# Score columns in token order, one store for four heads, masks on VectorE

## Chip, cores, metric

One core of one Trainium2 chip. The metric is the device time of the whole program in microseconds (us). A run over 1.5% above the fastest of its kernel in the same rounds is called slow, and ratios leave it out.

Engines are named as in the profile: PE is TensorE, PEld its weight load, DVE is VectorE, ACT ScalarE, POOL GpSimd. A store's landing is the time from its issue until its data has arrived. The granted clock is the share of TensorE's full clock that the chip allowed. In the traces it is 1.0 or 0.5 at any moment, and what is given is its mean over a stretch.

## The reference, cut to what matters

```python
# decode step with its gradients: B=2, one query token, 16 KV heads (32 query heads), 4096 keys, Dh=128
xn = layernorm(x)
scores = einsum("bhqd,bhkd->bhqk", q, k) * Dh ** -0.5      # q = xn @ wq
p = softmax(scores);  o = einsum("bhqk,bhkd->bhqd", p, v)   # then @ wo
out = x + attention(xn) + glu(xn)
# the outputs that weigh most: out_2 = dL/dk_cache and out_3 = dL/dv_cache,
# each [2, 16, 4096, 128] bf16; outer products of dscores (or p) with q (or do)
```

The KV caches are read (67 MB) and gradients of the same size are written (67 MB); with the weights and their gradients, 92.5 MB are read and 92.5 MB written.

## The kernel before

Sequence position is split as `(a j c4 cb)`: partition 32a + j of the natural load holds 32 tokens. The scores of the four heads of a group are built in one [128, 256] tile whose columns are (h, c4, j), since the matmul reads the transposed keys `X` at a step of 2 elements within a block of 32 columns j.

```python
def head_scores(src, t, b, g, l, s_ps):                 # t=0: K, t=1: V; l = head 0..3 of group g
    n = nat([P, NCH, Dh], "kv")
    nc.sync.dma_start(n[:].rearrange("p c d -> p (c d)"), src[b, G * g + l])
    X = xtile([P, NCH * Dh], "X")                        # two buffers
    t32(pairs(X[:]), pairs(n[:].rearrange("p c d -> p (c d)")))      # DVE 32x32 transpose, as fp32 pairs
    for be in range(4):
        for cq in range(4):
            nc.tensor.matmul(s_ps[:], lhsT=view(W[t][:], 0, P, (be * G + l) * WW + 24 - 8 * cq, [[1, P]]),
                rhs=view(X[:], 0, P, 2 * cq * Dh + 64 * (be // 2) + be % 2, [[Dh, 2], [8 * Dh, 4], [2, 32]]), ...)

def build_BD(st, b, t):                                  # block-diagonal right-hand sides, cut
    nc.scalar.copy(bd[:], bp[:]...)
    for c in range(4):
        nc.gpsimd.tensor_scalar(BD[t][:, c, :], bd[:], maskc[:, c:c + 1], None, op0=ALU.mult)

okview = out_2.rearrange("b h (a j c4 cb) d -> b h a c4 j (cb d)", a=4, j=32, c4=4)
def unit(A, cq):                                         # outer products: rows x BD, 128 x 1024 to "so"
    m["st"] = [stile([P, G, 8, Dh], "so") for _ in range(2)]          # 1 MB each, four buffers ("st")
    o = [ps_o(), ps_o()]
    ...                                                  # 4 matmuls K=32 into ps_o, evac by ACT or DVE
    if cq == 3:
        for aa in range(2):
            for l in range(G):
                nc.gpsimd.dma_start(oview[b, G * g + l, 2 * A + aa],
                                    m["st"][aa][:, l].rearrange("p c d -> p (c d)"))   # 256 KB
```

The buffers "st" also stage the weight gradients (stw, std, sto, stq). Rows of the softmax, `pr`, and of its gradient, `ds`, feed the outer products (as weights, columns as they stand) and, transposed to `pT` and `dsT`, the contractions with V and K.

## Time and profile before

| | before |
|---|---|
| time, median of the three runs before the prediction | 854.5 us (843 to 862) |
| PE / DVE / ACT / POOL busy | 72 / 42 / 38 / 42% |
| mean granted TensorE clock | 0.641 |
| a so store, issue to landing | 13.8 us (256 KB, 256 of them) |

The prediction below shows the main lines. One more pair will be needed: the span in 40 slices, busy tenths of PE and the granted clock in tenths.

```profile
PE   1885694797956896889786893867749677769532
...
PEclk9876567656775576755655576566866559575555
```

PE falls to 3 to 5 tenths in slices from end to end, and the clock moves between 0.5 and 0.8 in most of them.

### The profile page before, as it was taken

The page shows a single profiled execution, that of the slowest core. Times are in us where ns is not written, and L with a number is a line of the kernel's source. Part 1 is how long each engine was busy: PE and PEld are TensorE (multiplying, and loading weights), DVE is VectorE, ACT ScalarE, POOL GpSimd, SP SyncE. Part 2 cuts the span into 40 slices and gives each one's busy share as a digit, 9 for nine tenths or more (in the row PEclk, how much of TensorE's full clock was granted, in tenths as well). Part 3 has the DMA queues.
Part 4 walks back from the last instruction along what each step waited for, and adds up shares of the span by engine and source line. Part 5 has one row for each costly group of instructions (what it writes and reads, how often), then busy time and mean ns, then how long its engine had stood idle before and what let it go on. Part 6 is the DMA issues. An engine that isn't in the chain of part 4 may idle for free.

```text
span 852.4 us, 14847 instructions
## 1 busy us (share of the span) xinstructions
PE 613.6 (72%) x6297; PEld 306.8 (36%) x6297; DVE 355.2 (42%) x436; ACT 325.6 (38%) x436; POOL 357.1 (42%) x508
## 2 busy tenths in 40 slices
PE   1885694797956896889786893867749677769532
PEld 1543362434422452535242351423424234334100
DVE  8663134414553355324462253414435335352233
ACT  0243443363334444442343451343424434435330
POOL 4543152545334373635342372443536226434402
PEclk9876567656775576755655576566866559575555
DMA  9739598558948799688947798457975789456646
GB/s 314 271 122 246 177 272 277 117 168 255 363 138 266 214 347 300 140 257 264 291 147 214 182 355 265 74 164 251 324 208 157 235 236 329 140 127 135 131 115 155
DMA packets 105050, 186.32 MB, mean 219 GB/s; under 512 B 56300, under 2 KB 71288, under 8 KB 96792
## 3 DMA queue, kind: packets, MB, share of 16 engines
q0 software_dynamic: 76592, 92.89, 44.0%
q1 hardware_dynamic: 28392, 92.49, 29.5%
q8 instruction: 49, 0.80, 0.4%
q14 instruction: 17, 0.14, 0.0%
HBM read 92.48 MB, written 92.48 MB: 217 GB/s over the span
## 4 chain that ended last, share of the span: by engine, by line
DMA 45%; PE 27%; POOL 8%; ACT 8%; issue 5%; DVE 4%; SPq 1%; ACTq 0%; POOLq 0%; DVEq 0%
DMA out_dram<-so 41%; PE ps_o L511 8%; PE ps_sc L474 8%; ACT so L93 6%; POOL out_dram L519 6%; PE ps_m L487 3%; POOL BD L461 2%; DMA kv<-in_A_k_cache_dram 2%; DMA out_dram<-sto 1%; PE ps_m L496 1%; DMA wgu<-in_B_w_up_dram 1%; PE ps_o L379 1%; DVE X L102 1%; ACT std L93 1%; PE ps_m L297 1%
## 5 line engine op out<-in xcount | busy, mean ns | idle before, releaser
L93 ACT CAST so<-ps_o 128x1024 bf16<-128x1024 f32 x212 | 209.5, 1014 | 291.8 <-PE ps_o L511 143.9
L519 POOL DMA_DIRECT2D out_dram<-so x256 | 176.9, 698 | 149.2 <-ACT so L93 76.5
L474 PE MATMUL ps_sc<-X,W 128*128 128x256 bf16 x1024 | 205.9, 349 | 16.2 <-DVE X L102 10.8
L102 DVE STREAM_TRANSPOSE X<-kv 128x2048 f32<-128x2048 f32 x64 | 147.0, 2299 | 84.2 <-PE ps_sc L474 29.7
L474 PEld LDWEIGHTS <-W 128*128 128x128 bf16 x1024 | 108.6, 119 | 98.0 <-issue 65.7
L511 PE MATMUL ps_o<-BD,pr 32*128 32x512 bf16 x256 | 98.5, 559 | 51.1 <-ACT so L93 47.9
L461 POOL TENSOR_SCALAR BD<-bd,maskc 128x512 bf16<-128x512 bf16 x64 | 99.4, 1559 | 64.8 <-ACT bd L458 61.4
L511 PE MATMUL ps_o<-BD,ds 32*128 32x512 bf16 x256 | 86.7, 499 | 55.2 <-ACT so L93 44.8
L90 DVE CAST so<-ps_o 128x1024 bf16<-128x1024 f32 x44 | 53.4, 1214 | 71.7 <-PE ps_o L511 53.3
L379 PE MATMUL ps_o<-dyr,hb 32*128 32x288 bf16 x72 | 20.8, 394 | 46.0 <-ACT std L93 45.9
L511 PEld LDWEIGHTS <-ds 32*128 32x128 bf16 x256 | 15.4, 97 | 81.8 <-issue 78.8
L93 ACT CAST stw<-ps_o 128x1024 bf16<-128x1024 f32 x35 | 34.5, 1015 | 22.4 <-PE ps_o L345 20.8
L352 POOL DMA_DIRECT2D out_dram<-stw x18 | 14.3, 795 | 65.4 <-DMA out_dram<-so 33.6
L487 PE MATMUL ps_m<-kv,pT 128*32 128x128 bf16 x1024 | 40.8, 287 | 0.0
L93 ACT CAST std<-ps_o 128x576 bf16<-128x576 f32 x32 | 19.3, 641 | 56.3 <-DMA out_dram<-so 52.5
L511 PEld LDWEIGHTS <-pr 32*128 32x128 bf16 x256 | 15.5, 101 | 62.9 <-issue 56.0
L487 PEld LDWEIGHTS <-pT 128*32 128x32 bf16 x1024 | 23.5, 120 | 35.6 <-issue 33.9
L384 POOL DMA_DIRECT2D out_dram<-std x9 | 7.7, 859 | 56.5 <-ACT o_sb L490 21.8
L487 PE MATMUL ps_m<-kv,dsT 128*32 128x128 bf16 x1024 | 28.9, 283 | 1.9 <-ACT o_sb L490 1.7
L496 PEld LDWEIGHTS ps_m<-R,o_sb 128*128 128x128 f32 x128 | 24.6, 273 | 12.8 <-issue 10.5
L487 PEld LDWEIGHTS <-dsT 128*32 128x32 bf16 x1024 | 22.8, 127 | 17.4 <-issue 16.5
L496 PE MATMUL ps_m<-R,o_sb 128*128 128x2 f32 x128 | 26.9, 318 | 3.0 <-issue 3.0
(180 smaller groups left out, 575.5 us busy)
## 6 DMA issues: line engine op xcount, KB each, us to landing
out_dram<-so POOLq DMA_DIRECT2D x256, 256.0 KB, 13.8
kv<-in_A_k_cache_dram SPq DMA_DIRECT2D x32, 1024.0 KB, 11.1
kv<-in_A_v_cache_dram SPq DMA_DIRECT2D x32, 1024.0 KB, 11.7
out_dram<-stw POOLq DMA_DIRECT2D x18, 512.0 KB, 9.6
wd<-in_B_w_down_dram SPq DMA_DIRECT2D x9, 576.0 KB, 8.5
out_dram<-std POOLq DMA_DIRECT2D x9, 576.0 KB, 4.2
wo<-in_A_wo_dram SPq DMA_DIRECT2D x4, 1152.0 KB, 11.4
wgu<-in_B_w_gate_dram SPq DMA_DIRECT2D x9, 512.0 KB, 12.7
```

The lines of the kernel that those rows point to most:

```text
L90: nc.vector.tensor_copy(out=out, in_=in_)
L93: nc.scalar.copy(out, in_)
L102: nc.vector.transpose(out, in_)
L297: nc.tensor.matmul(dh[:], lhsT=Wdy[:, k, e, :], rhs=view(Xd[:], 0, P, 64 * k + e, [[D, FC], [2, 32]]), start=(k == 0 and e == 0), stop=(k ...
L352: nc.gpsimd.dma_start(out[0:512, f0:f0 + FS].rearrange("(c p) n -> p c n", p=P), st[:, 4 * w:4 * w + 4])
L379: nc.tensor.matmul(o[aa][:, k, 0:HD2], lhsT=hb[32 * a:32 * a + 32, 0, :], rhs=dyr[32 * a:32 * a + 32, k * HD2:(k + 1) * HD2], start=True, ...
L461: nc.gpsimd.tensor_scalar(BD[t][:, c, :], bd[:], maskc[:, c:c + 1], None, op0=ALU.mult)
L474: nc.tensor.matmul(s_ps[:], lhsT=view(W[t][:], 0, P, (be * G + l) * WW + 24 - 8 * cq, [[1, P]]), rhs=view(X[:], 0, P, 2 * cq * Dh + 64 * ( ...
L487: nc.tensor.matmul(o_ps[32 * cq:32 * cq + 32, :], lhsT=rowsT[:, 4 * h + c4, :], rhs=head[:, 8 * c4 + 2 * cq + h, :], start=(h == 0 and c4 ...
L496: nc.tensor.matmul(t_ps[:, 2 * l:2 * l + 2], lhsT=o_sb[:, l, :], rhs=R40[:, 2 * l:2 * l + 2], start=True, stop=True)
L511: nc.tensor.matmul(o[aa][:, h, :], lhsT=rows[32 * a:32 * a + 32, P * h:P * (h + 1)], rhs=BD[t][32 * a:32 * a + 32, cq, :], start=True, sto ...
L519: nc.gpsimd.dma_start(oview[b, G * g + l, 2 * A + aa], m["st"][aa][:, l].rearrange("p c d -> p (c d)"))
```

## The change

The intent: let the score columns stand in token order, so that row m of a staging tile is token block m. Then one DMA of 1 MB stores four heads ([128 partitions, 4 heads, 2 KB] on both sides), and 256 issues become 64. Token order is made by a strided matmul read for K and a strided transpose write for V. The block masks move from POOL to DVE. (`dve(1.2)` is no instruction: it tells the program's static balance, which shares the evacuations of PSUM between ACT and DVE, of the masks' time.)

```diff
-    okview = out_2.rearrange("b h (a j c4 cb) d -> b h a c4 j (cb d)", a=4, j=32, c4=4)
+    okview = out_2.rearrange("b h (a m cb) d -> b a m h (cb d)", a=4, m=P)       # ovview likewise
@@ build_BD
-            nc.gpsimd.tensor_scalar(BD[t][:, c, :], bd[:], maskc[:, c:c + 1], None, op0=ALU.mult)
+            nc.vector.tensor_scalar(BD[t][:, c, :], bd[:], maskc[:, c:c + 1], None, op0=ALU.mult)
+        dve(1.2)
@@ head_scores
-        t32(pairs(X[:]), pairs(n[:]...))
+        if t == 0:
+            t32(Xf, pairs(n[:]...))
+        else:
+            t32(view(Xf, 0, P, 0, [[1, 4], [P, 16], [4, 32]]), pairs(n[:]...))    # writes fp32 at step 4
-                    rhs=view(X[:], 0, P, ..., [[Dh, 2], [8 * Dh, 4], [2, 32]]),
+                if t == 0:                                                        # reads bf16 at step 8*Dh
+                    r = view(X[:], 0, P, ..., [[Dh, 2], [2, 32], [8 * Dh, 4]])
+                else:
+                    r = view(X[:], 0, P, ..., [[4 * P, 2], [2, P]])
@@ outer_units
-                        for l in range(G):
-                            nc.gpsimd.dma_start(oview[b, G * g + l, 2 * A + aa], m["st"][aa][:, l]...)
+                        nc.gpsimd.dma_start(oview[b, 2 * A + aa, :, G * g:G * g + G],
+                                            m["st"][aa][:].rearrange("p l c d -> p l (c d)"))
@@ softmax (and dscores likewise)
-        t32(pT[:]..., pr[:])
+        t32(pT[:]..., view(pr[:], 0, P, 0, [[P, 2], [1, 4], [4, 32]]))
```

## The prediction

> **What bounds the kernel now.** I read the page first, then the list of waits, then the stores one by one. Engine shares and DMA queues, from the page:
>
> ```profile
> PE 613.6 (72%) x6297; PEld 306.8 (36%) x6297; DVE 355.2 (42%) x436; ACT 325.6 (38%) x436; POOL 357.1 (42%) x508
> ...
> DMA packets 105050, 186.32 MB, mean 219 GB/s; under 512 B 56300, under 2 KB 71288, under 8 KB 96792
> ...
> q0 software_dynamic: 76592, 92.89, 44.0%
> q1 hardware_dynamic: 28392, 92.49, 29.5%
> ...
> DMA out_dram<-so 41%; PE ps_o L511 8%; PE ps_sc L474 8%; ACT so L93 6%; POOL out_dram L519 6%; PE ps_m L487 3%; POOL BD L461 2%; DMA kv<-in_A_k_cache_dram 2%; DMA out_dram<-sto 1%; PE ps_m L496 1%; DMA wgu<-in_B_w_up_dram 1%; PE ps_o L379 1%; DVE X L102 1%; ACT std L93 1%; PE ps_m L297 1%
> ```
>
> No engine is full. The last line is the chain of waits that ended last: 41% of the span (some 350 us) is the landing of the dK/dV stores from the tiles "so". Stores and loads move the same bytes, but the stores take half as much engine time again (44.0% against 29.5%). The list of waits says how this reaches TensorE:
>
> ```profile
> ACT so L93 <- DMA out_dram<-so: 102.4, 19, 13.4
> PE ps_o L511 <- ACT so L93: 92.7, 44, 12.3
> ACT std L93 <- DMA out_dram<-so: 52.5, 7, 11.4
> PE ps_o L379 <- ACT std L93: 45.9, 8, 10.8
> PE ps_o L647 <- ACT so L93: 13.6, 4, 11.6
> ```
>
> The 1 MB staging tiles have four buffers. ACT can't evacuate into one until its store has landed, so PSUM stays full and PE stands. PE's share of it is 92.7 + 45.9 + 13.6 = 152 us of its 239 us of idle (852.4 - 613.6).
>
> Why do the stores land so late? Two stretches answer it (columns: stretch, length, busy time of PE, PEld, DVE, ACT, POOL, granted clock, DMA busy share, GB/s). In the first only so stores were in flight; in the second mainly one stq store, of 1 MB as [128 partitions, 4 runs of 2 KB], which is the very shape that the change gives to so.
>
> ```profile
> 156.00:174.00 18.00, 12.52 (x105) 7.88 (x107) 6.42 (x11) 4.43 (x7) 8.91 (x15) 0.69 0.76 151
> 257.50:260.00 2.50, 2.50 (x17) 1.82 (x17) 1.43 (x3) 0.53 (x3) 2.14 (x4) 0.50 1.01 415
> ```
>
> Beside an idle load queue, so stores move 151 GB/s with the engines 76% busy; stq moves 415. Packet by packet, the 4 KB store packets take a steady 159 ns in the stq stretch; in the so stretch that is still the median, but many take 1 to 2 us. Of the 56300 small packets, 49152 are of 8 bytes, which is 256 so stores x 192, and 192 = 12 x 16: as if 12 of 16 engines got only filler from each so store. The issues agree:
>
> ```profile
> out_dram<-so POOLq DMA_DIRECT2D x256, 256.0 KB, 13.8
> out_dram<-stq POOLq DMA_DIRECT2D x4, 1024.0 KB, 6.7
> ```
>
> A quarter of the bytes takes twice as long. Eight so stores issued together at 154.3 us (2 MB, no loads) had all landed only at 174.9: 20.6 us.
>
> **What the Trainium skill says.** "DMA: Bandwidth & Descriptors", section "Why a DMA increments its semaphore by 16 and not by 1": a copy is spread over the largest k up to 16 that divides the slowest dimension of both patterns. Before, the DRAM side starts with c4 = 4, so k = 4; after, both sides start with 128, so k = 16. The filler count and the 151 against 415 GB/s agree. "SBUF — State Buffer", in "Door 1: The DMA port swizzle": SBUF lines are 16 bytes, and full bandwidth needs at least two hits in a line. K's new matmul read steps 2 KB in its innermost dimension and V's transpose write steps 16 bytes, so both get one. No instruction of the kernel before does either on a long operand, so its trace can't say. "VectorE: DVE Perf Modes", "The perf-mode tier table": tensor_scalar on bf16 in SBUF runs at four elements a cycle. "TensorE: Matmul & The Clock Gate", "Part 1: The HAM clock gate": an idle window of some 3.4 us halves the clock. The trace agrees: score matmuls start 111 ns apart (median) at clock 1.0 and 213 at 0.5, and the mean grant is 0.64.
>
> **The change part by part.** Rows that price it (line, engine, operation, tiles, shape, count, busy us, mean ns, idle before):
>
> ```profile
> L519 POOL DMA_DIRECT2D out_dram<-so x256 | 176.9, 698 | 149.2 <-ACT so L93 76.5
> L461 POOL TENSOR_SCALAR BD<-bd,maskc 128x512 bf16<-128x512 bf16 x64 | 99.4, 1559 | 64.8 <-ACT bd L458 61.4
> L623 POOL DMA_DIRECT2D out_dram<-stq x4 | 3.2, 797 | 5.0 <-DVE stq L90 2.8 <-DVE rowf L752 2.2
> L102 DVE STREAM_TRANSPOSE X<-kv 128x2048 f32<-128x2048 f32 x64 | 147.0, 2299 | 84.2 <-PE ps_sc L474 29.7
> L474 PE MATMUL ps_sc<-X,W 128*128 128x256 bf16 x1024 | 205.9, 349 | 16.2 <-DVE X L102 10.8
> ```
>
> Stores: 256 issues become 64 of 1 MB. POOL loses 256 x 0.698 = 179 us and gets 64 x 0.797 = 51. Landing: two tiles (2 MB) at 400 GB/s take 5.2 us, plus some 3 us of issue and completion: 8 to 9 us in place of 20.6 without loads, perhaps 12 beside them. The direct waits of ACT and DVE for landings add up to 213 us in 37 pieces (102.4, 52.5, 19.7, 16.2, 12.5, 10.1), 5.8 us each, so 10 us off the landing ends nearly all. I take 80% of PE's 152: -120 us.
>
> Masks: 64 x 1.559 = 99 us leave POOL, where stores stood behind them in its queue. On DVE a 128x128 bf16 copy takes 176 ns; another 384 columns at four a cycle add some 0.1, so 0.28 us, 18 us in all, off the path mostly: +5. POOL falls from 357 to about 130 us.
>
> K reads: 512 of the 1024 score matmuls. If one hit a line halves the rate, 213 ns is paid at full clock too. Of the consecutive pairs counted, 371 of 828 ran at clock 1.0: 512 x 0.45 x 0.1 = +23 us of PE.
>
> V writes: 32 transposes of 2.30 us. At half rate they add 32 x 2.2 = 70 us to DVE (42% busy). Mostly hidden; exposed perhaps at the first head of each of eight V phases, 8 x 2.2 = 18, at even odds: +10.
>
> The strided reads in pT and dsT cost nothing: the hT transpose already reads at step 4 (306 ns for 128 columns, against 428 for 256 contiguous).
>
> Clock: fewer long PE gaps should lift the grant from 0.64 to about 0.70. Half of PE's 613 us is rate rather than latency: -25 (estimate).
>
> Sum by PE idle: 854.5 - 120 - 25 + 23 + 10 + 5 = 748. This is the cautious end: it lets PE's busy time stand, though much of it is pipeline tail of matmuls trickling between waits. The chain gives the bold end: 350 us of landings shrink by 60% (-210), its POOL part (8%, 66 us) by 40 us, the costs add 38: 854.5 - 210 - 40 + 38 = 642. In between, leaning to the middle as other waits fill up part of what the chain frees: **695 us**.
>
> **The rivals.** (1) Transfers get no faster, since loads share the engines: landing stays at 10 us and above, gain some 40 us, 815. For it: 74% mean busy share. Against it: that share is mostly stretched packets, and the so stores are slow with no load beside them. (2) PE becomes the bound because K's 2 KB step costs far more than two cycles an element: at 4 times, 512 x 0.3 to 0.45 us = 150 to 230 us, and the result is about 850. Against it: the skill tells of a penalty per line, and a tuned kernel would hardly keep it. (3) DVE becomes the gate: POOL's masks waited 61.4 us for bd in nine waits; in DVE's fixed order (masks now stand between transposes) such a wait holds up the transposes that feed PE. With slow V writes too: 355 + 18 + 70 = 443 us busy, +40, 740. (4) Everything overlaps better and DMA is the floor: 186 MB at the 350 to 400 GB/s of the best stretches is 465 to 530 us, with start and tail of 50 to 70 us: 600.
>
> **Range and chances.** The store effect is measured in this kernel on the same shape, so faster is very likely. The spread comes from how much PE fills up (642 to 748) and from the strides. 80% range 615 to 785; faster by over 2%: 0.94, within 2%: 0.03, slower: 0.03.
>
> **What would show it.** Right: 8-byte packets gone (about 53,000 packets: 105050 - 49152 - 192 x 16), the store queue's share of engine time in us down by a quarter or more, so landing at 6 to 9 us, ACT's waits for landings under 60 us, POOL busy about 130 us, masks near 0.28 us, V transposes 2.3 to 4.6 us, K matmuls spaced at 213 ns at full clock. Wrong: landings still over 11 us (rival 1), K's matmuls above 400 ns apart (rival 2), or DVE waiting for bd while PE waits for X (rival 3).

## The result, and the profile after

The changed kernel took 883.3 us (median of 4 runs, 881.7 to 884.6) against 848.8 (4 runs): ratio 1.050, 95% interval 1.045 to 1.056. It is 5% slower; the prediction had said 695 us, 615 to 785. All ratios here are the mean time of one kernel's fast runs over the mean of the kernel before's fast runs of the same rounds, so they are not quite the ratio of the medians.

The page of the changed kernel, lines as in the prediction:

```profile
PE 798.6 (90%) x6297; PEld 324.7 (37%) x6297; DVE 406.3 (46%) x491; ACT 335.5 (38%) x445; POOL 129.3 (15%) x252
...
PE   2896999979999999979999999979999699997964
...
PEclk9855655565555555566655555556555655558555
...
DMA packets 52823, 185.89 MB, mean 211 GB/s; under 512 B 4076, under 2 KB 19064, under 8 KB 44568
...
q1 hardware_dynamic: 28392, 92.49, 29.6%
q0 software_dynamic: 24368, 92.48, 28.6%
...
PE ps_sc L484 31%; PE ps_o L520 18%; PE ps_m L496 6%; DVE X L102 6%; PE ps_m L505 3%; ACT so L93 3%; PE ps_o L379 2%; PE ps_m L297 2%; PE ps_o L655 2%; PE ps_o L345 1%; PE ps_m L253 1%; PE ps_m L417 1%; PE ps_m L284 1%; DMA out_dram<-so 1%; DVE so L90 1%
...
out_dram<-so POOLq DMA_DIRECT2D x64, 1024.0 KB, 6.3
```

The store side did all that was foretold. The 8-byte packets are gone (52,823 packets; I had written about 53,000), the store queue's engine time fell from 44.0% of 852 us = 375 us to 28.6% of 883 us = 252 us, and a store of four times the bytes lands in 6.3 us in place of 13.8. In the chain, landings fell from 41% to 1%. ACT's wait for them, 102.4 us before, is all but gone:

```profile
ACT so L93 <- DMA out_dram<-so: 2.7, 1, 2.7
```

But PE is now 90% busy, 185 us more than before, and stands at 9 tenths nearly everywhere, while its clock sits at 0.5: the mean grant fell from 0.641 to 0.574. PE's score matmuls head the chain. The groups (line, engine, operation, tiles, shape, count, busy us, mean ns of one, idle before):

```profile
L484 PE MATMUL ps_sc<-X,W 128*128 128x256 bf16 x1024 | 352.1, 491 | 28.2 <-DVE negb L544 14.9
L102 DVE STREAM_TRANSPOSE X<-kv 128x2048 f32<-128x2048 f32 x64 | 195.4, 3056 | 76.0 <-PE ps_sc L484 55.0
L527 POOL DMA_DIRECT2D out_dram<-so x64 | 48.8, 763 | 264.6 <-ACT so L93 144.7
```

The same 1024 score matmuls were busy for 205.9 us before and are for 352.1 now; the transposes rose from 147.0 to 195.4. The timeline shows single runs of 16 score matmuls, one head's K, without a wait inside (start, length, instruction): first two of the kernel before, at half and at full clock, then one of the changed kernel.

```profile
53.51 3.57 PE L474 MATMUL ps_sc<-X,W 128*128 128x256 bf16 x16 [1.03 <-DVE rz L543]
39.50 1.94 PE L474 MATMUL ps_sc<-X,W 128*128 128x256 bf16 x16
```
```profile
131.97 7.16 PE L484 MATMUL ps_sc<-X,W 128*128 128x256 bf16 x16
```

Over the whole trace, successive K matmuls start 437 ns apart (median), at clock 1.0 as well as at 0.5; V's still start 113 and 213 ns apart. So K's 2 KB step costs four times at full clock and twice at half. (The page counts a matmul's busy time with its pipeline, so its mean of 491 ns is longer than these distances.) V's transposes take a median of 3.81 us in place of 2.30.

**Theory A** after this: the store gain is whole; K's strided read alone costs more, directly (before, K matmuls ran 226 times at 111 and 193 times at 213 ns, mean 158, so 512 x (437 - 158) = 143 us) and by a lower clock for the rest. **Rival B**: PE at half clock is a bound of its own once no waits are left. **Rival C**: V's writes or the masks, both on DVE, gate PE.

### The profile page after: what moved, and what is told of

Its sections match the earlier page's. It is cut to its first block, busy times and chain, and to the rows that moved or that the text cites. A ratio compares the mean times of both kernels' runs of the same rounds, so it can differ in the third digit from the quotient of the medians.

```text
span 882.6 us, 14480 instructions
## 1 busy us (share of the span) xinstructions
PE 798.6 (90%) x6297; PEld 324.7 (37%) x6297; DVE 406.3 (46%) x491; ACT 335.5 (38%) x445; POOL 129.3 (15%) x252
## 2 busy tenths in 40 slices
DMA packets 52823, 185.89 MB, mean 211 GB/s; under 512 B 4076, under 2 KB 19064, under 8 KB 44568
## 3 DMA queue, kind: packets, MB, share of 16 engines
q0 software_dynamic: 24368, 92.48, 28.6%
## 4 chain that ended last, share of the span: by engine, by line
PE 73%; DVE 8%; issue 6%; ACT 3%; DMA 1%; POOL 0%; DVEq 0%; ACTq 0%; POOLq 0%
PE ps_sc L484 31%; PE ps_o L520 18%; PE ps_m L496 6%; DVE X L102 6%; PE ps_m L505 3%; ACT so L93 3%; PE ps_o L379 2%; PE ps_m L297 2%; PE ps_o L655 2%; PE ps_o L345 1%; PE ps_m L253 1%; PE ps_m L417 1%; PE ps_m L284 1%; DMA out_dram<-so 1%; DVE so L90 1%
## 5 line engine op out<-in xcount | busy, mean ns | idle before, releaser
L484 PE MATMUL ps_sc<-X,W 128*128 128x256 bf16 x1024 | 352.1, 491 | 28.2 <-DVE negb L544 14.9
L93 ACT CAST so<-ps_o 128x1024 bf16<-128x1024 f32 x222 | 219.8, 1014 | 280.3 <-PE ps_o L520 228.8
L102 DVE STREAM_TRANSPOSE X<-kv 128x2048 f32<-128x2048 f32 x64 | 195.4, 3056 | 76.0 <-PE ps_sc L484 55.0
L520 PE MATMUL ps_o<-BD,ds 32*128 32x512 bf16 x256 | 103.3, 602 | 8.2 <-ACT sto L93 2.6
L527 POOL DMA_DIRECT2D out_dram<-so x64 | 48.8, 763 | 264.6 <-ACT so L93 144.7
L90 DVE CAST so<-ps_o 128x1024 bf16<-128x1024 f32 x34 | 41.4, 1219 | 64.9 <-PE ps_o L520 41.9
L93 ACT CAST sto<-ps_o 128x576 bf16<-128x576 f32 x22 | 14.1, 639 | 47.7 <-PE ps_o L655 45.9
L102 DVE STREAM_TRANSPOSE Xw<-wgu 128x2304 f32<-128x2304 f32 x9 | 23.1, 2567 | 18.5 <-PE ps_sc L484 18.5
L102 DVE STREAM_TRANSPOSE Xd<-wd 128x1152 f32<-128x1152 f32 x9 | 12.4, 1373 | 37.2 <-PE ps_sc L484 37.2
L499 ACT COPY o_sb<-ps_m 128x128 f32<-128x128 f32 x64 | 17.0, 272 | 28.3 <-PE ps_m L496 28.0
```

The lines of the kernel that those rows point to most:

```text
L90: nc.vector.tensor_copy(out=out, in_=in_)
L93: nc.scalar.copy(out, in_)
L102: nc.vector.transpose(out, in_)
L499: nc.scalar.copy(o_sb[:, l, :], o_ps[:])
L520: nc.tensor.matmul(o[aa][:, h, :], lhsT=rows[32 * a:32 * a + 32, P * h:P * (h + 1)], rhs=BD[t][32 * a:32 * a + 32, cq, :], start=True, sto ...
L527: nc.gpsimd.dma_start(oview[b, 2 * A + aa, :, G * g:G * g + G], m["st"][aa][:].rearrange("p l c d -> p l (c d)"))
```

## The experiments

All ran against the kernel before on the same chip, 3 rounds if not said otherwise.

| run | what | time, us | ratio to before | PE busy | clock |
|---|---|---|---|---|---|
| changed kernel | | 883.3 | 1.050 | 798.6 | 0.574 |
| k_writes | K ordered by writes too | 739.2 | 0.868 | 622.1 | 0.671 |
| v_reads | V ordered by reads too | 1000.9 | 1.174 | 942.6 | 0.527 |
| late_order | order made on 256 columns | 678.2 | 0.795 | 583.4 | 0.704 |
| late_k_reads | late_order, K's reads back | 847.3 | 1.002 | 772.5 | 0.593 |
| late_v_writes | late_order, V's writes back | 720.8 | 0.849 | 608.7 | 0.675 |
| late_pool_masks | late_order, masks on POOL | 686.8 | 0.808 | (slow) | (slow) |
| late_head_stores | late_order, four stores a tile | 684.1 | 0.807 | (slow) | (slow) |
| before_split | before, 32-partition stores | 834.2 | 0.974 | 641.1 | 0.631 |
| before_spread | before, stores over 128 rows | 680.7 | 0.809 | 590.4 | 0.682 |
| late_four_engines | late_head_stores, stores over 4 | 823.1 | 0.978 | 635.8 | 0.618 |
| before_k_reads | before, K's reads | 946.9 | 1.128 | 793.1 | 0.591 |

Times are medians of all runs, ratios use fast runs alone. PE busy (us) and clock are of the profiled execution, and are left out where that was a slow run. The verdict on record is "unclear" for before_split, before_spread, late_four_engines and before_k_reads: in the rounds of the last three, on one chip, four of seven runs of the kernel before were slow. Their 95% intervals are 0.964 to 0.983, 0.799 to 0.819, 0.964 to 0.992 and 1.116 to 1.139, so the large effects (before_spread, before_k_reads) stand clear of noise, and the two near 0.975 are small gains at the edge of it. `steps` (one look) is told below.

The changed kernel, k_writes and v_reads have the same instructions in the same order on every engine, and so do late_order, late_k_reads and late_v_writes: within these two groups only access patterns differ.

### k_writes: K as V

```diff
-        if t == 0: t32(Xf, ...)
-        else:      t32(view(Xf, 0, P, 0, [[1, 4], [P, 16], [4, 32]]), ...)
+        t32(view(Xf, 0, P, 0, [[1, 4], [P, 16], [4, 32]]), ...)
-                if t == 0: r = view(X[:], ..., [[Dh, 2], [2, 32], [8 * Dh, 4]])
+                r = view(X[:], 0, P, 4 * P * 2 * cq + 2 * P * (be // 2) + be % 2, [[4 * P, 2], [2, P]])
```

> The changed kernel with K ordered as V is: by the transpose's strided write, with the matmul reading at step 2 again. Theory A (K's 2 KB step in the score matmuls is what costs): the 512 K matmuls fall from 437 ns apart to 113 to 213, PE busy falls by some 140 us or more, DVE gains 32 x 1.5 = 48 us; time 720 to 770. Rival B (PE at half clock is the bound as such, since the clock does not rise when PE is fed without gaps): time stays above 830. Rival C (strided transpose writes on DVE, or masks on DVE, gate PE): time stays about 880 or rises, with PE waiting for DVE X.

739 us, in Theory A's range. PE lost 176 us of busy time, DVE gained 46 (452.0), and the clock came back to 0.671. B and C as they stood are out: with PE fed without long gaps and all 64 transposes slow, the kernel is 13% faster than before.

### v_reads: V as K

```diff
-        else: t32(view(Xf, 0, P, 0, [[1, 4], [P, 16], [4, 32]]), ...)
+        t32(Xf, ...)
+                r = view(X[:], 0, P, 2 * cq * Dh + 64 * (be // 2) + be % 2, [[Dh, 2], [2, 32], [8 * Dh, 4]])
```

> The changed kernel with V ordered as K is: by strided matmul reads; no strided write on DVE. The suspected cost is doubled. Theory A: another 512 matmuls at 437 ns in place of 113 to 213: +130 to +160 us, time 1010 to 1050, clock share lower still. Rival B: the matmuls were slow anyway at half clock, +50 at most. Rival C (DVE gates): faster than 883, since 48 us leave DVE.

1001 us: +118 for the second 512 strided matmuls, net of the 43 us that leave DVE. That is 9 us below the range that A gave; its direction and size hold, and C, which wanted it faster, fails. The busy tenths of PE and its clock:

```profile
PE   2989999999999999999999999989999999999974
...
PEclk9555555555555555555555555555555555555555
```

PE is 94% busy and is granted half the clock from end to end.

### late_order: token order on 256 columns

Scores are left as before; what has to stand in token order is only the weight side of the outer products, `pr` and `ds`. One small copy each does it.

```diff
-        (the strided transpose write and the strided read; both as in the kernel before)
+        prt = small("prt", (P, 256), BF16)
+        nc.vector.tensor_copy(view(prt[:], 0, P, 0, [[P, 2], [1, 4], [4, 32]]),
+                              view(pr[:], 0, P, 0, [[P, 2], [32, 4], [1, 32]]))
-        outs += outer_units(pr, 1, b, g, ovview)
+        outs += outer_units(prt, 1, b, g, ovview)        # ds -> dst likewise; pT, dsT as before
```

> Scores, transposes and matmul reads as in the kernel before; token order is made by two small DVE copies of 256 columns an iteration (16 in all, some 0.4 us each), stores and masks as in the changed kernel. Theory A: all of the store gain and none of the stride cost: PE busy about 620 to 650, time 690 to 740, faster than k_writes by 10 to 40 us. Rival B: above 830. Rival C with masks on DVE as the gate: 800 or more, with PE waiting for DVE.

678 us, ratio 0.795 (0.789 to 0.800): faster than both kernels. The result is correct within the check's tolerance. (The softmax here is nearly flat, so the check would hardly see a wrong order of the rows of dV, out_3: before_spread below writes them in wrong places with an error of 0.006. It does see a wrong order of dK's rows: such runs miss out_2 by 1.4.)

```profile
PE 583.4 (86%) x6297; PEld 298.5 (44%) x6297; DVE 364.8 (54%) x507; ACT 331.3 (49%) x445; POOL 129.6 (19%) x252
...
PE   1679997798888999989888999989888999989954
...
PEclk9898559579686556778696556869796555885556
```

PE is nearly as dense as in the changed kernel, but clock slices of 8 and 9 are back, and the mean grant is 0.704, the value that the prediction had assumed. The 16 copies took 7.1 us of DVE in all.

### late_k_reads and late_v_writes: each part put back alone

```diff
 late_k_reads: late_order, in head_scores
+                if t == 0: r = view(X[:], ..., [[Dh, 2], [2, 32], [8 * Dh, 4]])
 late_v_writes: late_order, in head_scores
+        if t == 1: t32(view(Xf, 0, P, 0, [[1, 4], [P, 16], [4, 32]]), ...)   and V's read [[4 * P, 2], [2, P]]
```

> late_order with one part of the change put back: K's score matmuls read with the 2 KB step (the result is wrong on purpose: K's columns then stand in another order than the rest expects; the work is the same). Theory A (these reads alone turn the gain into a loss, directly and through the clock): 512 matmuls go from 113-213 ns to 437 ns: +130 us direct and some tens of us through the lower clock; time 830 to 880, mean clock below 0.60, against 678 and 0.70. Rival C (V's strided writes are a good half of the loss): below 790.

> late_order with the other part put back: V's transposes write with the 16-byte step and V's matmuls read that order at step 2 (wrong on purpose in the same way). 32 transposes at 3.8 in place of 2.3 us, 48 us of DVE. Theory A: mostly hidden, 690 to 715. Rival C: 760 or more, DVE X standing on the chain.

847 and 721 us. The score matmuls of late_order, then of late_k_reads, with all else alike:

```profile
L477 PE MATMUL ps_sc<-X,W 128*128 128x256 bf16 x1024 | 193.4, 331 | 12.6 <-DVE negb L543 7.5
L480 PE MATMUL ps_sc<-X,W 128*128 128x256 bf16 x1024 | 343.3, 480 | 10.4 <-DVE negb L546 7.5
```

K's reads cost +169, V's writes +43; 678 + 169 + 43 = 890, which is the changed kernel's 883 but for 7 us. Of the 169, 512 x (437 - 152) = 146 are direct (K's matmuls of late_order: 247 pairs at 111, 165 at 213, mean 152). That leaves 23 us, beside which the clock fell to 0.593: PE's other work was busy for 39 us more (583.4 - 193.4 = 390 before, 772.5 - 343.3 = 429 after), and PE's idle time fell by 24 us. Much of the half clock falls where it costs nothing, on K's matmuls, which take 437 ns at either clock: 97% of them start at half clock in late_k_reads and 41% in late_order; of the matmuls that are no scores, 75% and 56%.

V's writes: the +43 us is near the 48 us that the slower transposes add to DVE, slightly above A's 690 to 715 and far below C's 760. But PE's idle time grew by only 12 us (92.9 to 105.2), while its busy time grew by 25 at a lower clock (0.675), so how the DVE time reached the total is not shown.

### late_pool_masks and late_head_stores: the other two parts

```diff
 late_pool_masks: late_order
-            nc.vector.tensor_scalar(BD[t][:, c, :], ...)
-        dve(1.2)
+            nc.gpsimd.tensor_scalar(BD[t][:, c, :], ...)
 late_head_stores: late_order
-   nc.gpsimd.dma_start(oview[b, 2 * A + aa, :, G * g:G * g + G], m["st"][aa][:]...)         # 1 MB
+   for l in range(G):
+       nc.gpsimd.dma_start(oview[b, 2 * A + aa, :, G * g + l], m["st"][aa][:, l]...)        # 256 KB
```

> late_order with the masks back on POOL (64 x 1.56 us). If the masks on DVE are a side matter: within 10 us of late_order, 670 to 690. If masks in POOL's queue hold back stores and BD (which would explain that before_split gained only 2.6%): 730 to 800. If masks on DVE hurt: below 665.

> late_order with each staging tile stored by four DMAs of one head, 128 partitions and 256 KB (DRAM side starts with m = 128, so all 16 engines) in place of one of 1 MB. If spread over engines is what matters and not size: landing of the last of four within 2 us of late_order's 7.4, POOL busy +90 us but off the path, time within 2% of 678. If the number of issues matters (POOL's queue): 720 or more.

687 and 684 us; the ratios 0.808 and 0.807 stand 1.7 and 1.5% above late_order's 0.795. So what the change was named for, one store for four heads, and the masks on DVE are worth some 1 to 2% each, at the edge of what these runs can tell: they ran on another chip than late_order, and moving the masks also changed the static order and the balance of evacuations. Neither is the store gain.

### before_split, before_spread, late_four_engines: what the store gain is

```diff
 before_split: before, four DMAs of one c4 (32 partitions, four heads); rows right
+   for c in range(4):
+       nc.gpsimd.dma_start(oview[b, 2 * A + aa, c, :, G * g:G * g + G], m["st"][aa][32 * c:32 * c + 32]...)
 before_spread: before, only the DRAM rows; wrong rows on purpose
-   out_2.rearrange("b h (a j c4 cb) d -> b h a c4 j (cb d)", a=4, j=32, c4=4)
+   out_2.rearrange("b h (a m cb) d -> b h a m (cb d)", a=4, m=P)
 late_four_engines: late_head_stores, only the DRAM rows the other way; wrong rows on purpose
-   out_2.rearrange("b h (a m cb) d -> b a m h (cb d)", a=4, m=P)
+   out_2.rearrange("b h (a j c4 cb) d -> b h a c4 j (cb d)", a=4, j=32, c4=4)
```

> The kernel before with one thing changed: each 1 MB staging tile is stored as four DMAs of 32 partitions and four heads (DRAM side starts with j = 32) in place of four DMAs of one head and 128 partitions (DRAM side starts with c4 = 4). Same bytes, same 256 issues, no change of order. If the slowest dimension of 4 is what held the stores to 4 engines: the 8-byte packets vanish, landing falls from 13.8 to 6 to 9 us, time 720 to 780. If size or number of issues was the cause: landing stays near 13 us and the time within 2% of before.

> The kernel before with nothing changed but the DRAM side of the so stores: rows are written at token m = partition in place of (j, c4), so that the pattern starts with 128 and not with 4 (the rows of dK and dV then stand in the wrong places, on purpose). Same 256 issues of 256 KB, same static order of all engines, masks on POOL. If four engines a store are the whole bound of the kernel before: 8-byte packets gone, landing 5 to 8 us, time 680 to 720 (late_order has 678). If before_split's small gain of 2.6% is what spread alone is worth: 820 to 840. That would leave masks and size to explain the rest.

> late_head_stores (684 us) with nothing changed but the DRAM side of the so stores: (c4, j) as in the kernel before, so that it starts with 4 (rows in the wrong places, on purpose). Same static order. If the spread over engines is what the store gain rests on: 8-byte packets back (49152), landing 13 us or more, time 820 to 870. Otherwise: within 3% of 684.

before_split removed the 8-byte packets and landed in 5.5 us, and yet gained only 2.6%, which fitted neither expectation. Its instructions stand in another static order than before's: the stores' shape moved the scheduler. From one matmul of PE to the next the source line changes 676 times in place of 847, and 22 runs of 16 or more score matmuls stand in one piece in place of 9. PE then waits 35.2 us for DVE's X, where it was 10.8. That the order is all of it was not tested. For the landing it answers a rival: it keeps the spacing of the kernel before in DRAM, 8 KB from one row j to the next, and lands fast all the same, so it is not the scattered rows that made the landing slow.

before_spread is the clean form: the same instructions in the same order on every engine, only the first dimension of the DRAM pattern is 128 and not 4. It takes 681 us, ratio 0.809. late_four_engines is its mirror, again with an unchanged order, and gives the gain back: 823 us. Issues and queues of before_spread, then of late_four_engines:

```profile
q0 software_dynamic: 27440, 92.49, 36.9%
...
out_dram<-so POOLq DMA_DIRECT2D x256, 256.0 KB, 5.3
```
```profile
q0 software_dynamic: 76592, 92.89, 45.8%
...
out_dram<-so POOLq DMA_DIRECT2D x256, 256.0 KB, 13.5
```

76592 - 27440 = 49152, the 8-byte packets to the last one. So nearly all of the gain (ratio 0.809, where late_order has 0.795) comes from the first dimension of the pattern; it needs neither the larger stores nor the masks. That this dimension works by the number of DMA engines is the skill's rule that the prediction cites, and it fits the count of 12 x 16 small packets a store; these traces don't name the engine of a packet.

### steps: what a step costs

The kernel before (wrong on purpose), with K's matmuls of heads 0 to 3 reading at 4, 8, 16 and 32 bytes, and V's transposes writing at these steps; one look, state unknown, so only durations are used.

```diff
+   l == 1: rhs = view(X[:], 0, P, o, [[2048, 2], [4, 128]])    # 8 B;  l == 2: [8, 128], 16 B
+   l == 3: rhs = view(X[:], 0, P, o, [[512, 2], [16, 128]])    # 32 B
+   t == 1, l == 1: transpose to view(Xf, ..., [[1, 2], [64, 32], [2, 32]])    # 8 B; l == 2, 3: 16, 32 B
```

> A measurement, the result wrong on purpose: the kernel before, with the K score matmuls of heads 0 to 3 of each group reading at a step of 4, 8, 16 and 32 bytes, each at a source line of its own, and the V transposes of heads 0 to 3 writing at a step of 4, 8, 16 and 32 bytes. If an access costs by the 16-byte line: 4 bytes 111-213 ns apart by the clock, 8 bytes about 218 at either clock, 16 and 32 bytes 437; transposes 2.3 us at 4 and 8 bytes, 3.8 at 16 and 32. If it is the 2 KB step that is special: 16 and 32 bytes stay at 111-213. If cost grows evenly with the step: 32 bytes is far above 437.

Stretches of one head's 16 K matmuls at 8, 16 and 32 bytes (lines L488, L490, L492; 15, 14 and 10 of them in one piece) from the timeline, then the transposes at 8, 16 and 32 bytes (L474, L476, L478) from the groups:

```profile
330.52 3.58 PE L488 MATMUL ps_sc<-X,W 128*128 128x256 bf16 x15
338.04 6.48 PE L490 MATMUL ps_sc<-X,W 128*128 128x256 bf16 x14
345.42 4.76 PE L492 MATMUL ps_sc<-X,W 128*128 128x256 bf16 x10
```
```profile
L478 DVE STREAM_TRANSPOSE X<-kv 128x2048 f32<-128x2048 f32 x8 | 31.2, 3901 | 40.8 <-DMA kv<-in_A_v_cache_dram 27.7 <-PE ps_sc L486 13.1
L476 DVE STREAM_TRANSPOSE X<-kv 128x2048 f32<-128x2048 f32 x8 | 30.4, 3805 | 4.5 <-PE ps_sc L486 4.4
L474 DVE STREAM_TRANSPOSE X<-kv 128x2048 f32<-128x2048 f32 x8 | 18.4, 2303 | 6.1 <-PE ps_sc L486 6.1
```

Median distance of starts: 4 bytes 111 ns at full and 213 at half clock; 8 bytes 228 at both; 16 bytes 452; 32 bytes 460 (seen at half clock only); 2 KB 437 in the changed kernel. From 16 bytes up the cost hardly moves with the step; it goes by the 16-byte lines that a read touches: 452 ns / 256 = 1.77 ns a line at 16 bytes, 1.80 at 32, 1.71 at 2 KB, and 228 / 128 lines = 1.78 at 8. The transposes agree: 2.30 us at 4 and 8 bytes, 3.80 at 16; less the 0.17 us that a contiguous one takes beyond its 2048 cycles (2.13 us at the 0.96 GHz of the Trainium skill, "VectorE: DVE Perf Modes", "Specifications"), an estimate of (3.80 - 0.17) / 2048 = 1.77 ns a line.

### before_k_reads: the reads where PE has slack

```diff
-    rhs=view(X[:], ..., [[Dh, 2], [8 * Dh, 4], [2, 32]])
+    rhs=view(X[:], ..., [[Dh, 2], [2, 32], [8 * Dh, 4]] if t == 0 else [[Dh, 2], [8 * Dh, 4], [2, 32]])
```

> The kernel before with K's score matmuls reading at the 2 KB step and nothing else (wrong on purpose), same static order. Theory A: PE's 512 matmuls take 437 ns here too; part of the +140 to 170 us is hidden in the 150 us that PE stands waiting for stores: 900 to 970. If the strided read costs only where PE is the bound: within 3% of before.

947 us, +107 over the fast runs of the kernel before (839 on average in these rounds), where late_order paid +169 for the same edit. So some 60 us of it are hidden where PE stands waiting for slow stores, as A said. The changed kernel removed that hiding place in the same stroke as it added the cost.

## Why the prediction was wrong, step by step

- **Stores (-120 to -210).** Right in mechanism and in every sign named: packets, landing, queue, POOL 129.3 us (about 130 foretold), direct waits of ACT and DVE for landings 26 us (under 60). Measured alone, before_spread, the stores are worth 839 - 679 = 160 us (means of fast runs). The skill's rule on the slowest dimension (its page "DMA: Bandwidth & Descriptors") fits here to the packet. One reading was loose: the stretch of 151 GB/s held 38 packets of 4,608 bytes of another store beside the 614 of "so", and "many take 1 to 2 us" is 38 of 614 above 1 us; the argument does not change.
- **K reads (+23). This is the step that failed.** I took "at least two hits in a line" to mean that one hit halves the rate of full clock and costs nothing at half clock: 213 ns. The runs show 437 ns at either clock, and +169 us (late_k_reads). A line takes about 1.77 ns, so the old 4-byte read, four hits a line, was already at the edge: 64 lines x 1.77 = 113 ns, and it took 111 at full clock. The trace before showed that 111 ns, but nothing in it showed that fewer hits would be free or cheap; I put a guess of the size where only a measurement could stand. I had named K's matmuls above 400 ns apart, with a result of about 850 us, as rival 2 and set it aside because "a tuned kernel would hardly keep it", which is no evidence.
- **Clock (0.70, -25).** Wrong with it: 0.574. In late_order, without the strided reads, it is 0.704. The profiled executions with strided matmul reads stand at 0.527 to 0.606, lowest where PE is busiest (v_reads, 94%). Why the grant falls stays open. A low grant beside a busy PE does not even need strided reads: late_order's trace has PE busy for 56.8 of the 57.5 us from 361.5 to 419 us at a grant of 0.50. The thought behind this term was that fewer PE gaps lift the grant. That fits before_spread and late_order (0.682 and 0.704 against 0.641), but v_reads has the fewest gaps and the lowest grant, so it is no rule here. The trace before showed that the clock halves (111 and 213 ns), not what makes it halve. What is at stake in late_k_reads is at most the 39 us by which PE's other work grew.
- **V writes (+10).** The transposes' cost was in the range foretold (3.8 us each), but "mostly hidden" was wrong: +43 us on the time in late_v_writes, for 48 us of DVE.
- **Masks (+5).** 64 x 0.349 = 22 us on DVE, and the move is a small gain; rival 3 did not come true. Each mask took 0.349 us on average where 0.28 was foretold; the fastest of the 64 took 0.271.
- **The middle of two sums.** Without both stride costs (23 and 10) the prediction was 662 us; late_order took 678. One number that comes within 16 us supports the middle way between PE's idle time and the chain; it can't show that both sums were right, and some luck may be in it.

## What to carry to other kernels

Look at the first dimension of both sides of a DMA: a 4 there cost this kernel 19% of its time, and one edit of the DRAM pattern gave it back without larger transfers (with rows in wrong places; late_order is the form that is right). Put a permutation where the data is smallest: the same order cost 169 + 43 = 212 us on the 64 transposed K and V operands, and 7.1 us of DVE time on 16 tiles of 256 columns, with no cost seen in the total (late_order 678 us, before_spread, which orders nothing, 681). And before striding a hot operand, count its hits per 16-byte line, and measure one instruction, since a term that is "hidden in idle time" comes due when the same change removes the idle time.

## What the Trainium skill lacked or had wrong

- "SBUF — State Buffer", "Door 1: The DMA port swizzle": two hits a line are not enough for a bf16 matmul read at full clock. Two hits (8 bytes): 228 ns for 256 columns, against 111 with four. The size of the penalty for a TensorE read is on no page: about 1.77 ns a line (437 to 460 ns for 256 columns, from 16 bytes to 2 KB).
- "DMA: Bandwidth & Descriptors", "Why a DMA increments its semaphore by 16 and not by 1": the rule for k is right here, but the cost is not told: 151 against 415 GB/s in the trace before, 13.8 against 5.3 us of landing. Nor is the mark to look for: 192 packets of 8 bytes in each DMA with k = 4.
- "TensorE: Matmul & The Clock Gate", "Why this matters for your kernels": keeping TensorE busy for 4 us and more did not lift its clock here: v_reads' trace has PE busy for 175.9 of the 180 us from 260 to 440 us at a grant of 0.50, with strided reads, and late_order's for 56.8 of 57.5 us at 0.50, without them.
